# Where six parked tiles leave PSUM, and where the last transposes stand, in a backward pass of one decoder layer

## The chip, the core and the metric

The kernel runs on one core of a Trainium2 chip. The core has five engines with an instruction queue each: TensorE (PE in the profile; its weight loads are PEld), VectorE (DVE), ScalarE (ACT), GpSimd (POOL) and SyncE (SP). They work at the same time and wait for each other through semaphores. Data moves between HBM and the on-chip memory SBUF over 16 DMA engines; here GpSimd and SyncE issue the transfers. TensorE writes only to PSUM, which has 8 banks, and VectorE or ScalarE copy the results from there to SBUF.

The metric is the time of one execution on the device in microseconds, the median of several runs. Lower is better.

## What is computed

The reference is one decoder layer with adaptive layer norm (modulation by a condition vector `c`), attention of one token over the last 4096 positions of a key and value cache, and a gated feed-forward network (FFN); the kernel returns its output and the gradients of ten inputs, for a given output gradient.

```python
def forward(x, k_cache, v_cache, wq, wo, w_gate, w_up, w_down, c, w_mod):
    sa, ca, ga, sb, cb, gb = split6(silu(c) @ w_mod)          # w_mod: 1024 x 6144
    h = layernorm(x) * (1 + ca) + sa
    q = heads(h @ wq)                                         # 32 heads of 128; 4 key/value heads
    p = softmax(q @ k_window.T * 128 ** -0.5)                 # window of 4096 of 65536 positions
    x = x + ga * ((p @ v_window) @ wo)                        # wo: 4096 x 1024
    h = layernorm(x) * (1 + cb) + sb
    x = x + gb * ((sigmoid(h @ w_gate) * (h @ w_up)) @ w_down)  # 1024 -> 3584 -> 1024
    return x

out, grads = vjp(forward)(grad_out)
```

The gradients of the two caches are 64 MB each and zero outside the window, so the kernel has to write about 120 MB of zeros. The gradients of the weights are outer products of a column and a row: a row is broadcast over the 128 partitions once, and each tile of the gradient is that row times one column of scalars.

## The kernel before: the parts that matter

The kernel holds almost everything in one SBUF tile, `arena`, and `ar(offset, size)` is a piece of it, in KiB per partition. Eight matrices `B_t[0..7]` are computed early, from w_q, the attention state and w_o, and must be transposed for a later product (`dh1_ps`). Six of the transposed tiles stay in PSUM banks until the FFN is over ("parked"):

```python
    def park(p, pl, tag):
        BT_ps[p] = pl.tile([P, D], BF16, name="BT_ps", tag=tag)
        for i in range(KD):
            nc.tensor.transpose(BT_ps[p][:, i * P:(i + 1) * P], B_t[p][:, i * P:(i + 1) * P], ident_bf[:, :])
    # ... tiles 0 and 1 in banks "gu" and "x", 2 and 3 in the two of "na", 4 in "pq", 5 in "rq"
    rot[:] = [(psum, "mm")]       # until the end of the FFN, other work has this bank alone
```

`new_ps` and `new_tp` give the next bank of the list `rot` in turn. A side unit transposes one 128 x 1024 tile: eight transposes on TensorE into a bank, then one copy back by ScalarE. A list of such units, `jobs`, is run one by one between the operations of the FFN:

```python
    def tr_unit(blk, dst=None):
        def run():
            tp = new_tp("tp_side")
            for i in range(8):
                nc.tensor.transpose(tp[:, i * P:(i + 1) * P], blk[:, i * P:(i + 1) * P], ident_bf[:, :])
            nc.scalar.copy(out=blk if dst is None else dst, in_=tp[:, :])
        return run

    jobs[:] = [tr_unit(v_nat[:, i // 4, (i % 4) * 1024:(i % 4 + 1) * 1024]) for i in range(16)]
    side(3)
    # ...
    for h in range(HQ):
        jobs.append(tr_unit(wo_t[h // 4][:, h % 4, :]))
    jobs.append(tr_unit(B_t[7]))
    for g in range(G):
        jobs.append(tr_unit(N_sb[:, g * 1024:(g + 1) * 1024]))
```

The FFN's weights come in seven blocks (`NB` is 7). A block reduces each tile with `ttr` on VectorE (for the gradient of the normalized input), then overwrites it with its outer product on ScalarE (the weight's gradient) and stores it:

```python
    for q in range(NB):
        z = Z_FFN[q]
        more = q + 1 < NB
        for j in range(KD):
            w = ug_v[:, q % 2, j // 4, j % 4, :, :].rearrange("p k f -> p (k f)")
            ttr(w, w, dug_b, dh2acc[:, q * KD + j:q * KD + j + 1])
            if j in (0, 2, 5, 6):
                side()
            outer_act(w, h2[:, j:j + 1], dug_b)
            # ... at j == 0: ffn
            if j == 3:
                store_ug(q, 0, 4)
                zero(z[0])
            if j == 5:
                store_ug(q, 4, 2)
        store_ug(q, 6, 2)
        zero(z[1])
        if more:
            # ... front, gates and w_down's part of block q + 1, with three more side() calls
        else:
            zero(z[2] + z[3])
    side(len(jobs))
```

`ug_v` has two halves; odd and even blocks take turns, and the last block (number 6) leaves the odd half unused. Then the gradient goes back through the second layer norm to `dattn`, and through w_o:

```python
    B_t = [ar(o, 2) for o in (40, 42, 44, 152, 154, 156, 62, 60)]
    for p in range(6):
        nc.scalar.copy(out=B_t[p], in_=BT_ps[p][:, :])
    rot[:] = [(psum, "mm"), (pna, "na"), (pgu, "gu"), (ppq, "pq"), (px, "x"), (pna, "na"), (prq, "rq")]
    # ... dh2, dln2
    dx1b, m2 = layernorm_bwd_col(dln2, ln2, rstd2, "ln2b")     # means over partitions by a product on TensorE
    # ...
    mulv(dattn_bf, dx1, ga)
    bcast(dattn_bf, KD, dattn_b, "AV")
    # ...
    do4 = [new_ps("do4") for _ in range(2)]
    for b in range(2):
        for i in range(KD):
            for a in range(4):
                w = wo_t[4 * b + a].rearrange("p a (i d) -> p i a d", i=KD)
                nc.tensor.matmul(do4[b][32 * a:32 * a + 32, :], lhsT=dattn_bf[:, i:i + 1].broadcast_to([P, 32]),
                                 rhs=w[:, i, :, :], start=(i == 0), stop=(i == KD - 1), tile_position=(0, 32 * a))
        nc.scalar.copy(out=do_sb[b], in_=do4[b][:, :])
    # ... dh1_ps: 64 products with the transposed B_t
    def dwo(u):                                                # overwrites wo_t[u], which do4 reads
        for a in range(4):
            outer_dve(wo_t[u][:, a, :], o_col[:, 4 * u + a:4 * u + a + 1], dattn_b)
        nc.gpsimd.dma_start(out=wo_dram(out_5, u), in_=wo_t[u])
    # ... do_ps
    for u in range(4):
        dwo(u)
    bcast(dmod_bf[:, 16:48], 32, dmod_b4, "A")
    # ...
    dwo(4); dwo(5)
    # ... dq_ps: 32 products with the transposed N_sb, then dq_bf; dwo(6), sec(0); c_ps, crow
    sec(1)
    for tb in range(4):
        rebuild_P(tb)
    bcast(dq_bf, HQ, dq_b, "A")
    # ... dwo(7), sec(2), sec(3); dp_ps: products with the transposed v_nat; then
    # the gradients of V, w_q, w_mod and K, each tile stored by GpSimd as soon as it is made
```

In `bcast` each letter names the engine that copies half of the row out of PSUM, in turn: "A" ScalarE, "V" VectorE. `zero(n)` issues `n` stores of zeros, 1 MB each.

Of the kernel before, what the change touches and what calls it, by code (L numbers as in the profile page):

```python
# [20 lines left out]
KD = D // P  # L21
# [4 lines left out]
G = 4  # L26
# [32 lines left out]
def kernel(  # L59
# [26 lines left out]
    nc = tc.nc  # L86
# [13 lines left out]
    def ar(off, size):  # L100
        return arena[:, int(off * KIB):int((off + size) * KIB)]


    def vt(shape, name, dt=FP32):
        return pool.tile(shape, dt, name=name)
# [75 lines left out]
    def new_ps(name="ps"):  # L181
        p, tag = next_pool()
        return p.tile([P, 512], FP32, name=name, tag=tag)
# [4 lines left out]
    def new_tp(name="tp"):  # L188
        p, tag = next_pool()
        return p.tile([P, 1024], BF16, name=name, tag=tag)  # L190
# [7 lines left out]
    def addv(out, a, b):  # L198
        return tt(out, a, b, ALU.add)

    def cp(out, a):
        return nc.vector.tensor_copy(out=out, in_=a)  # L202
# [6 lines left out]
    def ttr(out, w, b, acc):  # L209
        return nc.vector.tensor_tensor_reduce(out=out, in0=w, in1=b, scale=1.0, scalar=0.0,  # L210
                                              op0=ALU.mult, op1=ALU.add, accum_out=acc)
# [28 lines left out]
    def outer_act(out, col, b):  # L240
        return nc.scalar.activation(out=out, in_=b, func=ACT.Copy, scale=col)  # L241
# [51 lines left out]
    def bcast(col_bf, ncols, out_bf, engs):  # L293
        for k, j0 in enumerate(range(0, ncols, 4)):
            ps = new_ps("bc_ps")
            for jj in range(4):
                nc.tensor.matmul(ps[:, jj * P:(jj + 1) * P],
                                 lhsT=col_bf[:, j0 + jj:j0 + jj + 1].broadcast_to([P, P]), rhs=ident_bf[:, :],
                                 start=(jj == 0), stop=(jj == 3), skip_group_check=True)
            o = out_bf[:, j0 * P:(j0 + 4) * P]  # L300
            if engs[k % len(engs)] == "A":
                last = nc.scalar.copy(out=o, in_=ps[:, :])
            else:
                last = cp(o, ps[:, :])
        return last
# [10 lines left out]
    v_nat = ar(96, 32).rearrange("p (g x) -> p g x", g=G)  # L316
    w01_T = ar(128, 16).rearrange("p (n j) -> p n j", n=KD)
    P_bf = ar(144, 8)
    N_sb = ar(144, 8)
# [9 lines left out]
    B_t = [junk if o is None else ar(o, 2) for o in B_off]  # L329
# [108 lines left out]
    jobs = []  # L438
# [5 lines left out]
    def side(n=1):  # L444
        for _ in range(n):
            if jobs:
                jobs.pop(0)()
# [332 lines left out]
    BT_ps = {}  # L780
# [51 lines left out]
# [7 lines that stand above are left out]
# [11 lines left out]
    def load_wd(q, s):  # L850
        nc.sync.dma_start(out=wd_v[:, 2 * s:2 * s + 2, :], in_=wd_dram(B_w_down, q, s))
# [14 lines left out]
    def store_ug(q, j0, n):  # L866
        for k, view in ((0, dwu_view), (1, dwg_view)):
            nc.gpsimd.dma_start(out=ug_part(view, q, j0, n), in_=ug_tile(q, k, j0, n))  # L868
# [42 lines left out]
    park(5, prq, "rq")  # L911
    tr_unit(B_t[6], ar(62, 2))()
    load_wd(0, 1)
    jobs[:] = [tr_unit(v_nat[:, i // 4, (i % 4) * 1024:(i % 4 + 1) * 1024]) for i in range(16)]
    side(3)
    mod_gb((4, 5))
    mulv(dffn_bf, go_col, gb)
# [22 lines left out]
    def gates(q):  # L940
        r, gu = small[q % 2], gu_t[q % 2]
        nc.scalar.activation(out=r["sg"], in_=gu[:, 0:4], func=ACT.Sigmoid)
        nc.scalar.activation(out=r["om"], in_=gu[:, 0:4], func=ACT.Sigmoid, scale=-1.0)
# [23 lines left out]
    def dug_part(q):  # L967
# [4 lines left out]
        for i in range(8):  # L972
            nc.tensor.transpose(tp[:, i * P:(i + 1) * P], r["dug_bf"][:, i:i + 1].broadcast_to([P, P]), ident_bf[:, :])
        nc.scalar.copy(out=dug_b.rearrange("p (s f j) -> p s f j", s=4, j=2),  # L974
                       in_=tp.rearrange("p (s j f) -> p s f j", s=4, j=2))

    for h in range(HQ):
        jobs.append(tr_unit(wo_t[h // 4][:, h % 4, :]))
    jobs.append(tr_unit(B_t[7]))
    for g in range(G):  # L980
        jobs.append(tr_unit(N_sb[:, g * 1024:(g + 1) * 1024]))

    front(0)
    gates(0)
# [11 lines left out]
# [3 lines that stand above are left out]
        for j in range(KD):  # L999
            w = ug_v[:, q % 2, j // 4, j % 4, :, :].rearrange("p k f -> p (k f)")  # L1000
            ttr(w, w, dug_b, dh2acc[:, q * KD + j:q * KD + j + 1])
            if j in (0, 2, 5, 6):
                side()
            outer_act(w, h2[:, j:j + 1], dug_b)
            if j == 0:
                if q == 0:
                    cp(ffn, ffn_ps)
                else:
                    addv(ffn, ffn, ffn_ps)
# [8 lines that stand above are left out]
            front(q + 1)  # L1018
            gates(q + 1)
            side()  # L1020
            hh_ops(q + 1)
            ffn_mm(q + 1, 0)
            wd_ttr(q + 1, 0)
            if q + 2 < NB:
                load_ug(q + 2, 0, 4)
            wd_outer(q + 1, 0)
            zero(z[2])
            if q + 2 < NB:
                load_ug(q + 2, 4, 2)
            side()  # L1030
            ffn_mm(q + 1, 1)
            wd_ttr(q + 1, 1)
            side()
            dug_part(q + 1)
            wd_outer(q + 1, 1)
            if q + 2 < NB:
                load_ug(q + 2, 6, 2)
            zero(z[3])
            if q + 2 < NB:
                load_wd(q + 2, 0)  # L1040
                load_wd(q + 2, 1)
        else:
            zero(z[2] + z[3])
    side(len(jobs))


    B_t = [ar(o, 2) for o in (40, 42, 44, 152, 154, 156, 62, 60)]
    for p in range(6):
        nc.scalar.copy(out=B_t[p], in_=BT_ps[p][:, :])
    rot[:] = [(psum, "mm"), (pna, "na"), (pgu, "gu"), (ppq, "pq"), (px, "x"), (pna, "na"), (prq, "rq")]  # L1050
    dh2 = vt([P, KD], "dh2")
    nc.vector.reduce_sum(out=dh2, in_=dh2acc.rearrange("p (b j) -> p j b", j=KD), axis=AX.X)
# [5 lines left out]
    dattn_bf = vt([P, KD], "dattn_bf", BF16)  # L1058
    mulv(dattn_bf, dx1, ga)
    dattn_b = b1k  # L1060
    bcast(dattn_bf, KD, dattn_b, "AV")
    dmod_bf = vt([P, KM], "dmod_bf", BF16)
    dgb = vt([P, KD], "dgb")
    mulv(dgb, go_col, ffn)
# [37 lines left out]
    def sec(j):  # L1102
        w5 = g_t[j] if j < 6 else sec_t[j][:, 3 * D:4 * D]
        ttr(w5, w5, dmod_b4[:, 3 * D:4 * D], dcs[:, j:j + 1])
        outer_dve(sec_t[j], cs_col[:, j:j + 1], dmod_b4)
        nc.gpsimd.dma_start(out=dwm_view[:, j, 2 * D:6 * D], in_=sec_t[j])
# [56 lines left out]
    for b in range(2):  # L1163
        for hh in range(4):
            nc.tensor.matmul(dov[:, b, :, hh], lhsT=do_sb[b][:, hh * P:(hh + 1) * P], rhs=ident_f[:, 0::32],
                             start=True, stop=True)
    for u in range(4):
        dwo(u)
    bcast(dmod_bf[:, 16:48], 32, dmod_b4, "A")
# [29 lines left out]
    crow = vt([P, 1], "crow")  # L1199
    cp(crow, c_ps[:, 0:1])  # L1200
    sec(1)
    for tb in range(4):
        rebuild_P(tb)
    bcast(dq_bf, HQ, dq_b, "A")
# [106 lines left out]
```

## Time and profile before

| | |
|---|---|
| time, median of 3 runs | 608.62 us (608.2 to 610.81) |
| span of the profiled run | 606.3 us |
| PE, DVE, ACT, POOL busy | 68%, 54%, 47%, 29% |
| bytes moved by DMA | 246.64 MB, mean 407 GB/s |
| HBM read, written | 60.30 MB, 185.60 MB |
| side units' copies by ScalarE (line 837) | 54, of 1009 ns each |
| copies of the six parked tiles (line 1049) | 6, of 1.05 us each |

The busy share of an engine is an average over the whole span, so it doesn't say which stage it limits. The profile also has the span in 40 equal slices, with the share of the DMA engines and the GB/s that they moved, windows of any stretch, and the chain of work that ended last, followed back from the end. "L241" is a line of the kernel, and can be that of a helper: L241 is `outer_act`, L206 the products and scalings of VectorE, L210 `ttr`, L836 and L837 the side units' transposes and copies, L1049 the copies of parked tiles, L1079 `do4`. A DMA share can be over 1, as packets overlap.

### The profile page before, as it was taken

The page shows a single profiled execution, that of the slowest core. Times are in us where ns is not written, and L with a number is a line of the kernel's source. Part 1 is how long each engine was busy: PE and PEld are TensorE (multiplying, and loading weights), DVE is VectorE, ACT ScalarE, POOL GpSimd, SP SyncE. Part 2 cuts the span into 40 slices and gives each one's busy share as a digit, 9 for nine tenths or more (in the row PEclk, how much of TensorE's full clock was granted, in tenths as well). Part 3 has the DMA queues.
Part 4 walks back from the last instruction along what each step waited for, and adds up shares of the span by engine and source line. Part 5 has one row for each costly group of instructions (what it writes and reads, how often), then busy time and mean ns, then how long its engine had stood idle before and what let it go on. Part 6 is the DMA issues. An engine that isn't in the chain of part 4 may idle for free.

```text
span 606.3 us, 11103 instructions
## 1 busy us (share of the span) xinstructions
PE 414.7 (68%) x4587; PEld 278.8 (46%) x4612; DVE 326.2 (54%) x619; ACT 285.4 (47%) x430; POOL 176.4 (29%) x283
## 2 busy tenths in 40 slices
PE   3997789999999989899964535435435356696300
PEld 3995333334344446546543424334434235596200
DVE  3754399999511020160006786685686528998440
ACT  3489514557201024212141875865866953595200
POOL 0002121222222212222331355445445404242230
PEclk9998599999999999999995555555555556755555
DMA  9999999999999999999999999999999998999996
GB/s 350 420 418 422 415 424 417 425 419 419 423 424 427 423 427 419 417 424 429 400 412 392 423 409 412 410 412 412 412 411 409 377 369 309 407 421 424 424 417 270
DMA packets 46899, 246.64 MB, mean 407 GB/s; under 512 B 5565, under 2 KB 5565, under 8 KB 26432
## 3 DMA queue, kind: packets, MB, share of 16 engines
q0 software_dynamic: 37824, 210.78, 91.0%
q1 hardware_dynamic: 8976, 35.14, 16.3%
q8 instruction: 36, 0.59, 0.4%
q14 instruction: 15, 0.12, 0.1%
q10 hardware_dynamic: 48, 0.01, 0.0%
HBM read 60.30 MB, written 185.60 MB: 406 GB/s over the span
## 4 chain that ended last, share of the span: by engine, by line
PE 43%; DMA 26%; DVE 13%; ACT 10%; issue 5%; POOL 0%; ACTq 0%; POOLq 0%; SPq 0%; DVEq 0%
PE b_ps L691 17%; DMA out_dram<-arena 13%; PE n_ps L636 6%; DMA arena<-in_B_w_down_dram 4%; DMA out_dram<-zeros 4%; ACT arena L241 4%; DVE arena L193 4%; DVE arena L206 3%; DMA arena<-in_w_mod_dram 3%; PE t_ps L598 2%; PE ps_kv L1138 2%; DVE arena L210 2%; PE tp_wq L453 2%; PE w_ps L394 1%; PE fold_ps L875 1%
## 5 line engine op out<-in xcount | busy, mean ns | idle before, releaser
L169 POOL DMA_DIRECT2D out_dram<-zeros x112 | 61.7, 553 | 195.7 <-PE q_ps L471 50.8
L691 PE MATMUL b_ps<-arena 128*128 128x512 bf16 x494 | 114.4, 381 | 1.2 <-issue 0.4
L836 PE MATMUL tp_side<-ident_bf,arena 128*128 128x128 bf16 x432 | 53.0, 300 | 59.7 <-ACT arena L837 51.6
L193 DVE TENSOR_TENSOR arena<-arena 128x2048 bf16<-128x2048 bf16 x64 | 76.5, 1223 | 2.3 <-PE n_ps L636 0.3
L691 PEld LDWEIGHTS <-arena 128*128 128x128 bf16 x512 | 49.1, 99 | 56.7 <-issue 4.5
L836 PEld LDWEIGHTS <-arena 128*128 128x128 bf16 x432 | 43.5, 138 | 65.4 <-issue 65.4
L837 ACT COPY arena<-tp_side 128x1024 bf16<-128x1024 bf16 x54 | 54.5, 1009 | 39.3 <-PE tp_side L836 38.9
L210 DVE CUSTOM_DVE_ANT_0 arena<-arena,scr 128x1024 bf16<-128x1024 bf16 x56 | 65.3, 1225 | 9.5 <-ACT scr L974 9.5
L636 PE MATMUL n_ps<-arena 128*128 128x512 bf16 x249 | 65.1, 378 | 6.9 <-DVE arena L193 5.0
L241 ACT ACTIVATE arena<-scr,h 128x1024 bf16<-128x1024 bf16 x56 | 61.3, 1146 | 0.0
L636 PEld LDWEIGHTS <-arena 128*128 128x128 bf16 x256 | 24.6, 97 | 41.6 <-issue 16.2
L868 POOL DMA_DIRECT2D out_dram<-arena x42 | 30.6, 732 | 44.6 <-ACT arena L241 32.9
L202 DVE CAST arena<-b_ps 128x512 bf16<-128x512 f32 x6 | 4.2, 692 | 62.8 <-PE b_ps L691 62.8
L1142 ACT ACTIVATE arena<-ps_kv 128x512 bf16<-128x512 f32 x48 | 26.1, 693 | 23.7 <-PE ps_kv L1138 23.4
L210 DVE CUSTOM_DVE_ANT_0 junk<-arena,b1k 128x1024 bf16<-128x1024 bf16 x28 | 34.3, 1224 | 5.0 <-DMA arena<-in_B_w_down_dram 4.5
L600 ACT CAST arena<-t_ps 128x512 bf16<-128x512 f32 x56 | 30.1, 589 | 12.1 <-PE t_ps L598 12.1
L1138 PE MATMUL ps_kv<-junk,arena 8*128 8x128 bf16 x256 | 27.1, 306 | 12.3 <-DVE arena L206 11.6
L1138 PEld LDWEIGHTS <-arena 8*128 8x128 bf16 x256 | 25.2, 142 | 14.0 <-issue 14.0
L455 ACT COPY arena<-tp_wq 128x1024 bf16<-128x1024 bf16 x23 | 21.8, 1030 | 8.6 <-PE tp_wq L453 8.6
L877 ACT CAST arena<-fold_ps 128x512 bf16<-128x512 f32 x16 | 9.4, 586 | 29.4 <-PE fold_ps L875 29.4
L954 PE MATMUL fg<-hh_bf,arena 128*128 128x1 bf16 x224 | 8.0, 166 | 19.6 <-DMA arena<-in_B_w_down_dram 17.8
L206 DVE TENSOR_SCALAR arena<-arena,cs_col 128x4096 bf16<-128x4096 bf16 (+1 forms) x16 | 16.0, 1017 | 8.9 <-DMA out_dram<-arena 8.8
(296 smaller groups left out, 649.6 us busy)
## 6 DMA issues: line engine op xcount, KB each, us to landing
out_dram<-zeros POOLq DMA_DIRECT2D x112, 1024.0 KB, 13.4
out_dram<-arena POOLq DMA_DIRECT2D x32, 1024.0 KB, 14.3
out_dram<-arena POOLq DMA_DIRECT2D x36, 512.0 KB, 8.9
arena<-in_A_wq_dram SPq DMA_DIRECT2D x8, 1024.0 KB, 19.9
out_dram<-zeros POOLq DMA_DIRECT2D x8, 960.0 KB, 12.5
arena<-in_w_mod_dram POOLq DMA_DIRECT2D x7, 1024.0 KB, 14.7
arena<-in_B_w_down_dram SPq DMA_DIRECT2D x14, 512.0 KB, 8.4
out_dram<-arena POOLq DMA_DIRECT2D x28, 256.0 KB, 9.3
```

The lines of the kernel that those rows point to most:

```text
L169: ins = nc.gpsimd.dma_start(out=region.bitcast(FP32), in_=zeros[:, :])
L193: return nc.vector.tensor_tensor(out=out, in0=a, in1=b, op=op)
L206: return nc.vector.tensor_scalar(out=out, in0=a, scalar1=s1, scalar2=None, op0=op0)
L210: return nc.vector.tensor_tensor_reduce(out=out, in0=w, in1=b, scale=1.0, scalar=0.0, op0=ALU.mult, op1=ALU.add, accum_out=acc)
L241: return nc.scalar.activation(out=out, in_=b, func=ACT.Copy, scale=col)
L600: nc.scalar.copy(out=o, in_=ps)
L636: mm = nc.tensor.matmul(nbank[k][:, :], lhsT=k_nat[:, g, t_ * DH:(t_ + 1) * DH], rhs=vp[:, t_ % 2, 4 * k:4 * k + 4, :].rearrange("p h d -> ...
L691: mm = nc.tensor.matmul(bbank[p][k][:, :], lhsT=a4[:, p, h, :], rhs=wo_t[u][:, a, k * 512:(k + 1) * 512], start=(i == 0 and a == 0), stop= ...
L836: nc.tensor.transpose(tp[:, i * P:(i + 1) * P], blk[:, i * P:(i + 1) * P], ident_bf[:, :])
L837: nc.scalar.copy(out=blk if dst is None else dst, in_=tp[:, :])
L868: nc.gpsimd.dma_start(out=ug_part(view, q, j0, n), in_=ug_tile(q, k, j0, n))
L1138: nc.tensor.matmul(ps[:, t4 * DH:(t4 + 1) * DH], lhsT=rows[32 * g:32 * g + HG, t_ * P:(t_ + 1) * P], rhs=hd[32 * g:32 * g + HG, :], start= ...
```

## The change

The last FFN block gets no side units. ScalarE copies the six parked tiles in their place, into homes in the half of `ug_v` that the last block leaves unused. So `jobs` must be empty by then: four of the 16 transposes of V move behind `c_ps`, ahead of `rebuild_P`, and the four of N move behind the w_o product, ahead of the first `dwo`. The broadcast of `dattn` is copied by VectorE alone. The aim is a shorter way from the last FFN block to the w_o product and the first gradient of w_o.

```diff
-    jobs[:] = [tr_unit(v_nat[:, i // 4, (i % 4) * 1024:(i % 4 + 1) * 1024]) for i in range(16)]
+    vT_unit = [tr_unit(v_nat[:, i // 4, (i % 4) * 1024:(i % 4 + 1) * 1024]) for i in range(16)]
+    jobs[:] = vT_unit[:12]
     side(3)
@@
+    jobs.append(tr_unit(B_t[7]))
     for h in range(HQ):
         jobs.append(tr_unit(wo_t[h // 4][:, h % 4, :]))
-    jobs.append(tr_unit(B_t[7]))
-    for g in range(G):
-        jobs.append(tr_unit(N_sb[:, g * 1024:(g + 1) * 1024]))
+    B_home = [ar(o, 2) for o in (24, 26, 28, 30, 40, 42, 62, 60)]
+
+    def unpark(p):
+        nc.scalar.copy(out=B_home[p], in_=BT_ps[p][:, :])
@@
             ttr(w, w, dug_b, dh2acc[:, q * KD + j:q * KD + j + 1])
-            if j in (0, 2, 5, 6):
+            if more and j in (0, 2, 5, 6):
                 side()
+            if not more and j in (0, 1, 2, 3, 5, 6):
+                unpark((0, 1, 2, 3, None, 4, 5)[j])
             outer_act(w, h2[:, j:j + 1], dug_b)
@@
-    side(len(jobs))
-
-
-    B_t = [ar(o, 2) for o in (40, 42, 44, 152, 154, 156, 62, 60)]
-    for p in range(6):
-        nc.scalar.copy(out=B_t[p], in_=BT_ps[p][:, :])
+    assert not jobs
+
+
+    B_t = B_home
@@
-    bcast(dattn_bf, KD, dattn_b, "AV")
+    bcast(dattn_bf, KD, dattn_b, "V")
@@ after do_ps, ahead of the first dwo
+    for g in range(G):
+        tr_unit(N_sb[:, g * 1024:(g + 1) * 1024])()
     for u in range(4):
         dwo(u)
@@ ahead of rebuild_P
     sec(1)
+    for run in vT_unit[12:]:
+        run()
     for tb in range(4):
         rebuild_P(tb)
```

## The prediction

> **What bounds the kernel now.** I read the page's slices first, then the windows around the one place where they dip, then the chain of waits through it, then ScalarE's timeline there. The slices (40 of 15.16 us each):
>
> ```profile
> PEclk9998599999999999999995555555555556755555
> DMA  9999999999999999999999999999999998999996
> GB/s 350 420 418 422 415 424 417 425 419 419 423 424 427 423 427 419 417 424 429 400 412 392 423 409 412 410 412 412 412 411 409 377 369 309 407 421 424 424 417 270
> ```
>
> The DMA engines are full from end to end, at 400 to 430 GB/s; no compute engine is (page: PE 68%, DVE 54%, ACT 47%). 246.64 MB at about 415 is 594 us of the 606.3 us span. So time can only be won where DMA is not full: slices 31 to 33 (377, 369, 309), about 470 to 515 us, and the ends. The same by stretches (columns: window, then busy us and count for PE, PEld, DVE, ACT, POOL, then granted clock, DMA share, GB/s):
>
> ```profile
> 460.00:475.70 15.70, 7.08 (x80) 5.89 (x81) 13.89 (x29) 9.78 (x12) 4.16 (x7) 0.50 1.11 419
> 475.70:478.00 2.30, 0.00 (x0) 0.00 (x0) 2.30 (x5) 2.30 (x4) 1.67 (x3) 0.50 0.62 228
> 478.00:498.30 20.30, 8.73 (x74) 6.40 (x77) 3.60 (x22) 14.14 (x15) 5.95 (x10) 0.50 1.11 412
> 498.30:502.40 4.10, 4.10 (x109) 2.62 (x101) 3.22 (x8) 1.17 (x2) 0.80 (x1) 0.98 0.00 0
> 502.40:520.00 17.60, 10.76 (x288) 10.18 (x288) 15.14 (x41) 6.13 (x11) 5.85 (x8) 0.58 1.00 365
> 520.00:560.00 40.00, 30.92 (x367) 27.23 (x359) 36.56 (x73) 29.00 (x55) 13.54 (x19) 0.59 1.04 422
> 560.00:600.00 40.00, 6.19 (x56) 5.65 (x55) 13.48 (x19) 4.18 (x7) 9.66 (x15) 0.50 1.01 418
> ```
>
> Two holes: a half-empty dip at 475.7 to 478.0, and 4.10 us with nothing moving (498.3 to 502.4). From 502.4 the share is 1.00, so 365 GB/s there is the speed of those stores (w_o gradients in 2 KB rows), not a third hole. From 520 to 600 DMA is full again. Why is the queue empty at 498.3? The chain of waits for this stretch (start us, us, what):
>
> ```profile
> 479.98 2.19 ACT arena L241 x2
> 482.17 0.91 ACT arena L837
> 483.12 1.03 PE tp_side L836 x8
> ...
> 487.34 1.03 PE tp_side L836 x8
> ...
> 489.30 5.61 ACT arena L1049 x6
> 494.95 1.01 PE bc_ps L297 x8
> 495.96 3.22 PE do L1079 x25
> 499.18 6.79 DVE arena L206 x16
> ```
>
> Block 6's outer products (L241) end at about 482.1. Then four leftover side transposes go one by one through the single bank "mm" (PE 1.03, copy 1.0 each), then six parked tiles leave their banks (L1049), then dattn's broadcast, the w_o product (`do4`, L1079), and only then VectorE may overwrite `wo_t[0]`. Its first store goes out at 501.15 (GpSimd's timeline: 14.56 us idle before it). Meanwhile the five zero stores issued at 483.91 to 486.6 last until 498.3. VectorE's timeline shows what this delays: it ends `ln2b_parts` at 478.98 and gets the means' product only at 488.72, because that small product stands behind the side transposes in PE's order; `dattn_bf` is ready at 489.87, and its broadcast waits until 494.95 because the next buffer in rotation is "rq", the bank of parked tile 5, copied last.
>
> **What the Trainium skill says.** "DMA: Bandwidth & Descriptors", section "Anatomy of one DMA — SWDGE (gpsimd) path": the DMA engines never wait on semaphores; the wait is on the issuing sequencer, and the engines work through what is queued. The trace agrees: GpSimd idles 14.56 us, but DMA is empty only 4.10, the queued zeros covering the rest. "TensorE: Matmul & The Clock Gate", section "What you observe": the clock doubles after about 4 us of sustained matmuls. Here it is 0.5 until the w_o product and 1.0 from about 498.5, after 3.5 us of it: 32 matmuls took 3.22 us, the next 32 about 1.6. "SBUF — State Buffer", section "SBUF: two separate sides": VectorE's two-port modes can keep GpSimd from writing descriptors. Here issues beside VectorE's w_o products took 0.75 to 0.85 us (0.53 to 0.56 for most zero stores), so no long block is visible.
>
> **The change part by part.**
>
> (a) Six copies move into block 6 at j = 0, 1, 2, 3, 5, 6, in place of the four side copies (j = 0, 2, 5, 6). A copy takes 5.61/6 = 0.935 us of ScalarE's time, an outer product 1.045 (3.23 for three, less overlap). Before: ScalarE waits for the first side transpose, starts outer 0 at 470.86, ends outer 3 at about 475.95, and the first gradient store issues at 476.33. After: the first copy needs no PE and starts when `dug_b` is written (468.8), ends 469.7; outer 0 then waits for VectorE's reduction of the same tile (ends 470.04), so starts near 470.15. Up to the end of outer 3 come 4 x 1.045 + 3 x 0.935 = 7.0, so 477.1 in place of 475.95. All three stores of the block come about 1.2 us later (477.5, 480.5, 483.6). The first lies at the dip: DMA is already half empty at 476, so it stays empty longer. Cost on DMA: about +1.1 us. The homes (24 to 30, 40, 42 KiB) held block 5, whose stores issued by 458.6 for these tiles land about 9 us later (page, DMA issues), before 468.8: no wait there.
>
> (b) Gone after block 6: the queue of four side units (482.1 to 489.3, 7.2 us) and six copies (5.6 us). The means' product can run at 479.0; 489.87 - 488.72 = 1.15 us of VectorE gives `dattn_bf` at about 480.8 (was 489.87). Building both kernels and counting buffer rotation, I find the two broadcasts on "na" and "rq"; "rq" is freed by the sixth copy at about 481.1, so nearly no wait. Both broadcast copies now go to VectorE (0.69 each), since ScalarE is busy to 483.2: about 482.8. The product starts near 481.9, cold: 3.3 us for the half that `dwo(0)` waits for. First `dwo` at about 485.2 instead of 499.18: **14 us earlier**. First w_o store near 487.2 instead of 501.15.
>
> (c) The zeros then last to about 498.3 + 1.1 = 499.4, with w_o stores queued since 487. The 4.10 us hole closes: -4.1 us.
>
> (d) Added behind the product: four N units, PE about 1 us and copy 0.935 each, now over several banks: 3.7 us of ScalarE before the dmod broadcast; and four V units ahead of `rebuild_P`, another 3.7. They delay the q-gradient by about 2 us and P by about 4 to 7, while this side is 14 us ahead, so it stays 7 to 12 us ahead of DMA. The 365 GB/s stores hold DMA for 17 us there. No time.
>
> Sum: -4.1 + 1.1 = **-3.0 us**, 608.6 to 605.6; I say 605.5. The 14 us of shorter chain is not the gain: 10 of it lie under zeros which had to be written anyway.
>
> **Rivals.**
>
> Rival 1, the chain counts in full. If 502 to 600 were paced by VectorE, ScalarE and PE, the whole part would move 10 to 14 us: 595 to 598. For it: the page's chain gives PE 43% and DMA only 26%. Against it: from 520 to 600 the DMA share is 1.01 to 1.04, bytes are unchanged, and after 556 GpSimd's timeline shows nearly every issue waiting about 1.9 us for an earlier store. I give it under one in twenty.
>
> Rival 2, the hole comes back later. The added 7.5 us of ScalarE, or the reuse of buffers (the dV tiles need w_o stores landed; the dwq tiles need the early stores landed) could empty the queue between 505 and 535. Then 607 to 609. For it: in-order VectorE and GpSimd, so one late item holds all behind it. Against it: by my count 10 us of data lie ahead of every such wait.
>
> Rival 3, the dip at 476 grows more than I think, because the six copies lengthen block 6, each maybe 1.05 us instead of 0.935, or wait for a store of block 5. At +2 to 3 us the gain shrinks to 1 or 2: 606.5 to 607.5.
>
> Rival 4, the dip does not grow: without side transposes ScalarE starts earlier, and the zero stores ahead cover it: then 604.5.
>
> **Range and chances.** The hole is a firm 4.1; the dip's growth is 0 to 2.5; other shifts of DMA mixing perhaps 1 either way; the three runs of before spread over 608.2 to 610.81. So 603.5 to 607.6. A gain over 2% means below 596.4, which needs rival 1; a loss over 2% would need 12 us of new holes, and nothing in the profile offers that. Chances: 0.03, 0.95, 0.02.
>
> **What would show it.** Right: a DMA window without zero throughput near 498 to 502; the first w_o product of VectorE near 485; the first gradient store of block 6 near 477.5 and a longer dip around 476 to 479; last DMA near 598 instead of 601. Wrong: a new window with low DMA share between 505 and 540 (rival 2); ScalarE's unparking copies with idle time before them waiting on DMA (rival 3); a span shorter by over 8 us with DMA's rate from 520 on above 430 GB/s (rival 1).

## The result, and the profile after

| | before | after |
|---|---|---|
| time, median of 6 runs each | 609.15 us (608.2 to 610.81) | 605.12 us (604.65 to 606.18) |
| ratio, with its 95% interval | | 0.9934 [0.9917, 0.9952] |
| span of the profiled run | 606.3 us | 604.4 us |

The change gains 4.0 us by the medians; the prediction said 605.5 us, 3.1 less than the 608.6 that the kernel before then had. The profiled run of the changed kernel is one of its two slowest (606.17 us), that of before its fastest (608.13 us), so the two traces show only 1.9 of the 4.0 us. I therefore compare them stretch by stretch, and not by their ends.

The page's slices of the changed kernel, each now 15.11 us:

```profile
PEclk9998899999999979979995555555555596755555
DMA  8999999999999999999999999999999999999995
GB/s 351 420 417 421 414 425 417 420 415 420 422 424 425 422 429 419 407 428 414 399 416 398 365 409 415 408 409 414 408 409 414 378 424 413 418 427 424 424 417 226
```

Slices 31 to 33 (counted from 0; about 468 to 514 us) have 378, 424 and 413 GB/s, where before had 377, 369 and 309. Slice 31, the dip in block 6, stayed; the other two were mended. Slice 22 is worse (365 against 423), which is taken up below. Three stretches of the kernel before, then the changed kernel (columns as before: window, busy us and count for PE, PEld, DVE, ACT, POOL, then clock, DMA share, GB/s):

```profile
476.00:484.00 8.00, 2.90 (x24) 2.54 (x24) 2.88 (x9) 7.02 (x8) 5.03 (x8) 0.50 0.95 346
498.00:503.00 5.00, 5.00 (x118) 3.38 (x111) 3.82 (x10) 1.17 (x2) 0.94 (x2) 0.95 0.14 49
503.00:519.00 16.00, 9.16 (x241) 8.58 (x244) 13.54 (x37) 5.13 (x10) 5.70 (x8) 0.57 1.01 365
```

```profile
476.00:484.00 8.00, 2.02 (x18) 1.47 (x22) 6.37 (x20) 8.00 (x9) 3.50 (x5) 0.50 0.94 342
484.00:498.00 14.00, 13.06 (x240) 9.67 (x233) 12.76 (x39) 7.43 (x11) 8.55 (x12) 0.91 1.13 421
498.00:503.00 5.00, 2.03 (x74) 1.76 (x71) 3.07 (x8) 2.25 (x5) 1.56 (x2) 0.71 1.10 415
503.00:519.00 16.00, 12.12 (x234) 9.16 (x234) 13.11 (x35) 11.35 (x16) 4.82 (x6) 0.77 1.04 415
598.00:606.00 8.00, 0.00 (x0) 0.00 (x0) 0.00 (x0) 0.00 (x0) 0.00 (x0) 0.50 0.03 13
```

Two things are to be seen. The hole is gone: 415 GB/s at 498 to 503, where the same window of before moved 49. And the w_o stores at 503 to 519 run at 415, where they ran at 365. The prediction had the first; it took the 365 for the speed of those stores and so had no gain there.

The table turns such windows into time. For each stretch it takes the difference of the rate to that of before, times the length of the stretch, divided by the 422 GB/s that a full stretch moves: the us that a kernel gained on before in that stretch. The gains come from the bytes themselves; from the rounded rates they can differ by 0.2 us in the longest stretches. Four kernels of the experiments stand beside it.

| stretch, us | before, GB/s | after | block 6 only (4) | copies behind block 6 (3) | zero earlier (9) | both (12) |
|---|---|---|---|---|---|---|
| 196 to 324 | 419 | -1.0 | +0.1 | -0.2 | +0.2 | -0.2 |
| 324 to 348 | 407 | -1.6 | -0.9 | -0.9 | -0.6 | -0.8 |
| 348 to 476 (two windows) | 410, 416 | +0.3 | +0.5 | +0.5 | +0.5 | +0.3 |
| 476 to 484, the dip | 346 | -0.1 | -3.4 | +0.9 | +0.9 | +1.5 |
| 484 to 498 | 427 | -0.2 | -1.5 | -0.1 | -0.3 | -0.2 |
| 498 to 503, the hole | 49 | +4.3 | +4.4 | +4.3 | +4.3 | +4.3 |
| 503 to 519, w_o stores | 365 | +1.9 | -0.1 | +2.0 | +2.0 | +2.0 |
| 519 to 590 (three windows) | 418, 423, 422 | +0.1 | -0.1 | -1.9 | 0.0 | +0.1 |

So the changed part, 476 to 519 us, gained 5.9 us: 4.3 by the hole, 1.9 by the rate behind it, -0.3 in block 6 and the stretch after it. From 519 to 590 nothing changed: both kernels are full there. Two losses stand against the 5.9 us in this trace. One is 2.7 us ahead of 348 us. Up to there all kernels of this document but number 6 run the same instructions in the same order, and yet 324 to 348 moves between 353 and 413 GB/s in their traces: variation from run to run, not a cost of the change. The other is the end. After 598 us the changed kernel has almost nothing left to move, but its last packets arrive at 601.6 us: 13 GB/s in the window above, at a DMA share of 0.03, which is half of one of the 16 engines. Before still moved 155 GB/s there and ended at 603.6 us. When 244 of the 246.64 MB have landed, the changed kernel is 3.5 us ahead of before; at the last packet 2.0 are left.

How the compute side moved is seen in the chain of waits of the changed kernel (start us, us, what):

```profile
480.74 0.60 PE tot_ln2b_means L255 x2
...
482.57 1.03 PE bc_ps L297 x8
483.61 4.98 PE do L1082 x57
...
492.07 0.48 PE tp_side L836 x8
492.57 3.76 ACT arena L837 x4
```

The side units and the six copies that stood between block 6 and the broadcast are gone. From the means in VectorE's hands (481.36 in its timeline) to the w_o product (L1082, the former L1079, at 483.61) are 2.2 us, where it was 7.2, from 488.72 to 495.96. VectorE's timeline has its first product for `dwo(0)` at 486.90, where before it was 499.18. The N units (L836, L837) stand behind.

The dip in block 6 is seen in ScalarE's timeline of the changed kernel (start, us, engine, line, operation, tiles, count, idle time before and its releaser):

```profile
470.46 1.02 ACT L984 COPY arena<-BT_ps 128x1024 bf16<-128x1024 bf16 x1
471.86 1.15 ACT L241 ACTIVATE arena<-scr,h 128x1024 bf16<-128x1024 bf16 x1 [0.39 <-DVE dh2acc L210]
472.92 0.99 ACT L984 COPY arena<-BT_ps 128x1024 bf16<-128x1024 bf16 x1
473.81 1.15 ACT L241 ACTIVATE arena<-scr,h 128x1024 bf16<-128x1024 bf16 x1
474.86 1.00 ACT L984 COPY arena<-BT_ps 128x1024 bf16<-128x1024 bf16 x1
475.75 1.15 ACT L241 ACTIVATE arena<-scr,h 128x1024 bf16<-128x1024 bf16 x1
476.80 1.01 ACT L984 COPY arena<-BT_ps 128x1024 bf16<-128x1024 bf16 x1
477.69 2.20 ACT L241 ACTIVATE arena<-scr,h 128x1024 bf16<-128x1024 bf16 x2
...
482.62 2.21 ACT L241 ACTIVATE arena<-scr,h 128x1024 bf16<-128x1024 bf16 x2
```

Copies (L984) and outer products (L241) alternate at 1.94 us a pair, so the first four outer products end at about 478.8 and the first gradient store of the block goes out at 479.15; before, it went out at 476.33. GpSimd's timelines, before and after:

```profile
476.33 1.52 POOL L868 DMA_DIRECT2D out_dram<-arena  x2 [7.45 <-ACT arena L241]
479.15 1.52 POOL L868 DMA_DIRECT2D out_dram<-arena  x2 [8.56 <-ACT arena L241]
```

### The profile page after: what moved, and what is told of

The parts are those of the page before. It is cut to its first block, busy times and chain, and to the rows that moved or that the text cites. A ratio compares the mean times of both kernels' runs of the same rounds, so it can differ in the third digit from the quotient of the medians.

```text
span 604.4 us, 11129 instructions
## 1 busy us (share of the span) xinstructions
PE 415.3 (69%) x4612; PEld 275.5 (46%) x4612; DVE 327.1 (54%) x620; ACT 284.5 (47%) x429; POOL 175.9 (29%) x283
## 2 busy tenths in 40 slices
DMA packets 46899, 246.64 MB, mean 408 GB/s; under 512 B 5565, under 2 KB 5565, under 8 KB 26432
## 4 chain that ended last, share of the span: by engine, by line
PE 36%; DMA 28%; DVE 15%; ACT 8%; issue 8%; POOL 1%; ACTq 0%; POOLq 0%; SPq 0%; DVEq 0%
PE b_ps L691 14%; DMA out_dram<-arena 14%; DVE junk L210 4%; DVE arena L206 3%; ACT arena L241 3%; DMA arena<-in_B_w_down_dram 3%; DMA out_dram<-zeros 3%; DMA arena<-in_w_mod_dram 3%; DMA arena<-in_A_wo_dram 3%; PE n_ps L636 3%; ACT arena L837 2%; DVE arena L210 2%; PE tp_wq L453 2%; PE tp_side L836 2%; DVE arena L193 2%
## 5 line engine op out<-in xcount | busy, mean ns | idle before, releaser
L691 PE MATMUL b_ps<-arena 128*128 128x512 bf16 x512 | 122.4, 393 | 0.7 <-DMA arena<-in_A_wo_dram 0.7
L836 PE MATMUL tp_side<-ident_bf,arena 128*128 128x128 bf16 x432 | 50.9, 297 | 47.4 <-ACT arena L837 40.5
L837 ACT COPY arena<-tp_side 128x1024 bf16<-128x1024 bf16 x54 | 54.0, 1012 | 41.9 <-PE tp_side L836 41.6
L836 PEld LDWEIGHTS <-arena 128*128 128x128 bf16 x432 | 42.3, 137 | 51.9 <-issue 51.7
L241 ACT ACTIVATE arena<-scr,h 128x1024 bf16<-128x1024 bf16 x56 | 61.6, 1147 | 0.4 <-DVE dh2acc L210 0.4
```

Of the source, the lines that this page charges most:

```text
L691: mm = nc.tensor.matmul(bbank[p][k][:, :], lhsT=a4[:, p, h, :], rhs=wo_t[u][:, a, k * 512:(k + 1) * 512], start=(i == 0 and a == 0), stop= ...
```

## Experiments

Each kernel was compared with the kernel before on the same chip; the medians of before were 609.12 us beside numbers 1 to 4, 609.63 beside 5 to 8, 609.29 beside 9 to 11 and 609.2 beside 12. Numbers 7, 8, 10 and 11 have one run each, the others 4 to 19. My theory at first: the time follows from the holes in DMA's work alone, the 365 GB/s behind the hole included, as a consequence of it. Against it stood rival 1 (the earlier compute is worth something by itself) and the reading of the prediction (365 GB/s is the speed of those stores).

### 1. The hole filled with zeros, the compute left late

Two zero stores of the end are issued ahead of the hole instead of behind it (three there instead of one); nothing else changes.

```diff
-Z_END = (1, 1, 1, 0, 0)
+Z_END = (3, 0, 0, 0, 0)
```

> The kernel before with two 1 MB zero stores moved from behind the first w_o stores to ahead of them (three instead of one); no compute instruction moves. Theory (only DMA idle time sets the end): two stores of 2.45 us fill the hole of 4.10 us at 498 to 502, so -4 us if nothing opens later; the two stores are then missing at 511 and 522, so up to 2 or 3 us may come back near 530: 604 to 607 against 609. If the 365 GB/s of the w_o stores came from the hole and not from their rows, they run at about 410 here too, and 2 us more are won. Rival (the chain of PE, ScalarE and VectorE after the FFN paces the end): no change, 609.

Measured: 608.01 us (605.61 to 610.66), ratio 0.9972 [0.9947, 0.9997]; 604 to 607 was expected. Its windows:

```profile
498.00:503.00 5.00, 5.00 (x115) 2.86 (x105) 3.23 (x9) 1.17 (x2) 0.80 (x1) 0.85 1.15 428
503.00:519.00 16.00, 9.53 (x213) 9.21 (x213) 13.40 (x37) 4.11 (x9) 5.20 (x7) 0.71 1.01 369
532.00:548.00 16.00, 13.98 (x178) 12.76 (x178) 15.96 (x21) 13.05 (x27) 5.46 (x8) 0.55 0.83 322
```

The hole is full (428), which is worth 4.5 us at that place, but only 1 to 2 us are left at the end (1.1 by the medians, 1.7 by the ratio). At 532 to 548 a new hole opens (322): the zeros that lay there before are gone, and the compute, 12 us later than in the changed kernel, can't fill it. From 519 to 590 this kernel loses 6.1 us to before, 3.8 of it in that hole. So closing a hole needs both: something to move now, and compute that is early enough when the moved zeros are missed. And the 365 stayed (369) though no full hole lies ahead of it: that part of my theory fell as I had put it.

### 2. The changed kernel, with the hole made again

The zeros of the last block are issued behind the w_o products instead. The compute is as early as in the changed kernel.

```diff
-Z_FFN = [(1, 1, 0, 1)] * 5 + [(1, 1, 1, 1), (1, 2, 1, 1)]
-Z_END = (1, 1, 1, 0, 0)
+Z_FFN = [(1, 1, 0, 1)] * 5 + [(1, 1, 1, 1), (0, 0, 0, 0)]
+Z_END = (0, 7, 1, 0, 0)
```

> The changed kernel with six zero stores moved from ahead of the first w_o store to behind the sixth one; compute is untouched, so the w_o products still start near 487. Theory (the gain is what the early w_o stores and the queued zeros keep DMA from being idle): DMA runs empty between block 6's stores and the first w_o store, 4 to 5 us of holes in all, so 608 to 610, nearly all of the gain lost, and the w_o stores drop to about 365 GB/s again if a hole ahead of them is the cause of that. Rival (the shorter chain is the gain): it stays at 605.

Measured: 610.6 us (609.89 to 612.5), ratio 1.0022 [1.0014, 1.003]. The whole gain is lost, with compute as early as it was. Windows:

```profile
476.00:492.00 16.00, 9.98 (x165) 7.03 (x166) 13.72 (x43) 10.03 (x11) 6.19 (x9) 0.71 0.75 267
492.00:504.00 12.00, 7.67 (x161) 7.32 (x158) 9.57 (x26) 7.68 (x12) 6.25 (x10) 0.65 1.00 355
504.00:520.00 16.00, 7.93 (x181) 7.38 (x182) 7.75 (x24) 7.74 (x9) 3.96 (x7) 0.61 1.13 419
```

The changed kernel moves about 380 GB/s in the first of these (342 for 8 us, 421 for the other 8): (380 - 267) x 16 / 422 = 4.3 us lost in the hole, and (420 - 355) x 12 / 422 = 1.8 us in the slow stretch behind it; 6.1 in sum, 5.5 by the medians. Rival 1 is refuted: 12 us of earlier compute are worth nothing where DMA runs dry. And the slow w_o stores are back, in a kernel that otherwise has them fast.

### 3. The copies behind block 6, the side units still moved away

The opposite half of the change: the six tiles leave their banks after the block, as before, while the N and V units stay behind.

```diff
-            if not more and j in (0, 1, 2, 3, 5, 6):
-                unpark((0, 1, 2, 3, None, 4, 5)[j])
@@
+    for p in range(6):
+        unpark(p)
     B_t = B_home
```

> The changed kernel with the six copies of parked tiles taken out of block 6 and put behind it on ScalarE, as before; no side units in block 6 either, so its ScalarE work is the eight outer products alone. Theory (DMA): the block's first gradient store issues about 4 us earlier than in the changed kernel, so the dip near 480 (about 1.4 us) nearly goes, and the first w_o product about 2 us later costs nothing: 603.5 to 605 against 605.1. Rival (chain): about 2 us slower than the changed kernel, 607.

Measured: 602.95 us (602.59 to 603.09), ratio 0.9891 [0.9875, 0.9908], better than the changed kernel, outside its interval, and better than the 603.5 to 605 expected. ScalarE's timeline in this kernel:

```profile
471.00 9.24 ACT L241 ACTIVATE arena<-scr,h 128x1024 bf16<-128x1024 bf16 x8 [1.30 <-DVE dh2acc L210]
480.15 5.56 ACT L984 COPY arena<-BT_ps 128x1024 bf16<-128x1024 bf16 x6
```

Eight outer products in one go; the first store of the block issues at 475.95 instead of 479.15, and 476 to 484 moves 395 GB/s, where it was 342: 1.0 us. The first w_o product comes at 489.91, three us later than in the changed kernel, and the hole stays closed with 410. What it loses is later, 1.9 us over 519 to 590 in the table: 0.8 at 532 to 548 (401 GB/s), where the compute is only just early enough, and 1.0 at 556 to 590 (409 GB/s, before 422), where the DMA share is 1.01 in both. So the copies inside the block, the most visible part of the change, cost; by number 4 what gains is that the side units left the way (together with the broadcast's copies by VectorE alone, which was not tried by itself). The dip explains 1.0 of the 2.2 us between the medians. The trace's other differences lie ahead of 348 us and at the end, and I can't tell there what is cause and what is variation.

### 4. The copies inside block 6 alone

The kernel before, with the copies taken into block 6 and the side units left where they were, between and behind.

```diff
             if j in (0, 2, 5, 6):
                 side()
+            if not more and j in (0, 1, 2, 3, 5, 6):
+                unpark((0, 1, 2, 3, None, 4, 5)[j])
@@
-    B_t = [ar(o, 2) for o in (40, 42, 44, 152, 154, 156, 62, 60)]
-    for p in range(6):
-        nc.scalar.copy(out=B_t[p], in_=BT_ps[p][:, :])
+    B_t = B_home
```

> The kernel before with only one part of the change: the six copies inside block 6, but the side units stay where they were (four in block 6, four after it). Theory (DMA): block 6's first store comes 3 to 4 us later, so the dip at 476 grows by about as much; the way to the first w_o product is about as long as before, so the hole stays at 2 to 4 us: 609 to 612. Rival (moving the copies is what helps): below 607.

Measured: 609.89 us (608.64 to 611.61), ratio 1.0016 [1.0005, 1.0027]. Windows:

```profile
476.00:484.00 8.00, 2.02 (x16) 1.69 (x16) 3.46 (x11) 8.00 (x9) 2.07 (x3) 0.50 0.47 165
503.00:519.00 16.00, 11.11 (x231) 10.85 (x231) 13.21 (x38) 4.36 (x9) 6.21 (x9) 0.66 1.00 362
```

Here ScalarE is packed: its first store of the block goes out at 480.56, the dip falls to 165 GB/s, and the hole at 498 to 503 is closed only because the zeros behind the block are late as well (issued from 489.81, before from 483.91). The table shows it as a trade: 4.9 us lost in 476 to 498, 4.4 won in the hole, and the w_o stores as slow as before. Half of the change alone is worth nothing.

### 5. The copies in the order in which the banks are needed

Number 3, with the tiles copied so that the banks of the first broadcasts come free first.

```diff
-    for p in range(6):
+    for p in (2, 5, 3, 0, 4, 1):
         unpark(p)
```

> The version with the six copies behind block 6 (602.95), with the copies reordered to parked tiles 2, 5, 3, 0, 4, 1, so that the two banks which dattn's broadcast takes next are free first (there the broadcast waited until 483.02 and 485.76). Theory: the first w_o product comes 3 to 4 us earlier (486 to 487), and the slower stretch of stores near 532 to 548, where the compute had run late, goes: 601 to 602.5. Rival (behind the closed hole nothing of the chain matters any more): no change, 603.

Measured: 603.19 us (602.87 to 604.09), ratio 0.9897 [0.9873, 0.992], the same as number 3, as the rival had it. The broadcast stands at 481.42 and the w_o product at 482.39, and 532 to 548 is mended (423 GB/s, 401 in number 3), and when 244 of the 246.64 MB have landed this kernel is 1.8 us ahead of number 3. But its last 0.25 MB take from 594.7 to 598.3 us, those of number 3 from 596.4 to 598.5. In these two traces what was won in the middle is lost in the last packets. The cause of that end is not settled.

### 6. Number 5, with zeros moved from the middle into the fold

`Z_FOLD` counts the zero stores around the start of FFN block 0: three of them move from behind its first stores to ahead of its first product.

```diff
-Z_FOLD = (0, 4, 3)
+Z_FOLD = (0, 7, 0)
```

> The same as e5, and the three zero stores that follow FFN block 0's first stores are issued ahead of its first product instead. Theory: the weak place at 330 to 336 (the changed kernel's profile shows 145 GB/s in its worst 2 us) is a dry queue before those zeros, so 1 to 2 us less than e5. Rival (the zeros only move, and the queue runs dry at the next store): the same as e5.

Measured: 603.98 us (603.64 to 605.23), ratio 0.9908 [0.9887, 0.9929]: no gain. It was aimed at the weak stretch around 330 us. 328 to 336 rises to 427 GB/s (311 in number 5), but 340 to 344 falls to 244 (415) and 344 to 348 to 314 (404). The hole was only moved, as the rival said.

### 7. Number 2, with the w_o stores issued late (inconclusive)

Meant to let six w_o stores go out in one burst after the last product, so that they run without VectorE's products beside them.

```diff
-        nc.gpsimd.dma_start(out=wo_dram(out_5, u), in_=wo_t[u])
+        if u > 5:
+            nc.gpsimd.dma_start(out=wo_dram(out_5, u), in_=wo_t[u])
@@ behind dwo(5)
+    for u in range(6):
+        nc.gpsimd.dma_start(out=wo_dram(out_5, u), in_=wo_t[u])
```

> The starved version (e2) with the first six w_o stores all issued when the sixth is computed, so that none of them runs while VectorE makes those products; the queue has been dry for some 10 us by then. If the slow w_o stores (365 GB/s in place of 410) come from a queue that ran dry just ahead of them, they are slow here too, about 355 to 370. If they come from VectorE's products running at the same time, they are fast, 405 to 420. The time itself is some 10 us above e2 by the longer hole.

Measured: 610.6 us in one run. Each store still left when its own tile was ready (488.40, 490.10 and so on), since GpSimd had nothing else to wait for: the edit didn't do what it was for, and the run is a repeat of number 2, with 355 to 358 GB/s in the slow stretch. Number 10 does it properly.

### 8. The changed kernel, with 24 products more on VectorE

Is it VectorE's work in SBUF that slows the stores? The 24 products have the form of the w_o products, write to a free place and add nothing to the result.

```diff
     dwo(5)
+    for u in range(24):
+        outer_dve(ar(44, 2), o_col[:, u:u + 1], dattn_b)
```

> The changed kernel with 24 more VectorE products of 128x1024 into an unused piece of SBUF behind the sixth w_o product (about 10 us of VectorE's time, at 498 to 508), so that the w_o stores, which run from 500 on with a full queue, have the same VectorE work beside them as in the kernel before. If that work makes the stores slow: 355 to 370 GB/s from 500 on. If a dry queue does: 405 to 420. The time: within 1 us of the changed kernel if there is 10 us of room behind the hole, up to 5 us more if not.

Measured: 605.36 us in one run. Windows:

```profile
476.00:484.00 8.00, 2.89 (x26) 1.81 (x30) 6.34 (x23) 7.95 (x9) 3.50 (x5) 0.50 0.87 312
500.00:508.00 8.00, 0.00 (x0) 0.00 (x0) 7.43 (x17) 1.72 (x4) 0.29 (x1) 0.56 1.02 412
536.00:540.00 4.00, 4.00 (x44) 4.00 (x43) 4.00 (x5) 4.00 (x9) 2.13 (x3) 0.50 0.73 295
```

VectorE is busy 93% of 500 to 508 with nothing but such products, and the w_o stores run at 412 GB/s beside them. So the products don't slow the stores. The third window shows the room that was left: delayed by some 10 us, the compute no longer keeps up at 536 to 540. The first is a second trace of the changed kernel's dip, as the two kernels are the same up to `dwo(5)`: 312 GB/s here, 342 there.

### 9. The changed kernel, with one zero store earlier

The dip from the other side: one zero store moves from behind block 6 to the end of block 5, ahead of block 6's stores.

```diff
-Z_FFN = [(1, 1, 0, 1)] * 5 + [(1, 1, 1, 1), (1, 2, 1, 1)]
+Z_FFN = [(1, 1, 0, 1)] * 5 + [(1, 1, 1, 2), (1, 1, 1, 1)]
```

> The changed kernel with one 1 MB zero store moved from behind block 6 to ahead of it (behind block 5's last stores). Theory (the dip near 479 to 483, about 1.4 us, is the queue running dry before block 6's late first store): 2.45 us more in the queue close it, 603.5 to 604.2 against 605.1, while the backlog behind block 6 is still long enough. Rival (what is won there is lost again at the end, where single DMA engines finish late): 605.

Measured: 602.67 us (602.24 to 603.87), ratio 0.9894 [0.9875, 0.9912]. The window of the dip:

```profile
476.00:484.00 8.00, 3.40 (x30) 2.04 (x34) 6.27 (x26) 7.44 (x8) 3.75 (x6) 0.50 1.06 395
```

395 GB/s for 342: 1.0 us by bytes, and 2.4 us by the medians, more than I expected. Nothing about the copies was changed, so the dip is a matter of what is queued ahead of the late stores. In its trace the last byte lands at 597.8 us, 3.8 us ahead of the one trace of the changed kernel. By the table 2.2 of these lie ahead of 348 us, where the two kernels are the same, and 1.0 in the dip, so this pair of traces can't say where the rest of the 2.4 comes from.

### 10. Number 2, with the first w_o stores held until the products are done

The proper form of number 7: the first of the six stores also waits for the last product of `dwo(5)`.

```diff
+            prod = outer_dve(wo_t[u][:, a, :], o_col[:, 4 * u + a:4 * u + a + 1], dattn_b)
@@ behind dwo(5), in place of the stores inside dwo
+    for u in range(6):
+        st = nc.gpsimd.dma_start(out=wo_dram(out_5, u), in_=wo_t[u])
+        if u == 0:
+            dep(st, last_prod)
```

> What e7 was meant to do: the starved version (e2), with the first six w_o stores held until VectorE has made the sixth product (in e7 each still went out as soon as its own tile was ready), so none of them runs beside those products. Dry queue ahead makes them slow: 355 to 370 GB/s from about 498 to 514. VectorE's products make them slow: 405 to 420. The time is 7 to 9 us above e2 by the longer hole.

Measured: 620.01 us in one run. DMA is dry from 491 to 499 us (2 GB/s). Then:

```profile
500.00:516.00 16.00, 9.81 (x268) 9.07 (x268) 12.29 (x32) 9.56 (x14) 6.96 (x11) 0.68 1.00 364
517.00:525.00 8.00, 5.83 (x55) 2.96 (x51) 7.93 (x14) 5.26 (x11) 1.61 (x2) 0.80 1.14 424
```

The products for these stores are all done when the first one leaves, six stores are issued together, and they run at 364 GB/s all the same. Neither the products nor the pace of the issue makes them slow. VectorE has other work meanwhile (12.29 of the 16 us), but number 8 shows fast stores beside a busier VectorE. With the next zeros the rate is 424.

### 11. Number 2, with one zero store among the w_o stores

```diff
-Z_END = (0, 7, 1, 0, 0)
+Z_END = (0, 6, 1, 0, 0)
@@
         dwo(u)
+        if u == 0:
+            zero(1)
```

> The starved version (e2) with one of its zero stores put right behind the first w_o store. In the kernel before, in e1, e2 and e4 the slow stores went on until a zero store came up. If one zero store ends it: from about 495 on 405 to 420 GB/s, and about 1.5 us less than e2 (609). If it needs a long queue: still 355 to 370 until the later zeros.

Measured: 608.71 us in one run. Windows:

```profile
490.00:492.00 2.00, 2.00 (x30) 2.00 (x30) 2.00 (x6) 0.45 (x1) 1.09 (x2) 0.98 1.03 369
494.00:506.00 12.00, 7.11 (x158) 6.78 (x156) 9.10 (x24) 5.92 (x11) 4.76 (x8) 0.64 1.02 406
```

The first store runs at 369, then the zero passes (442 at 492 to 494), and the w_o stores that follow it run at 406. One zero store ends the slow stretch. The expectation counts number 1 among the cases, wrongly: no zero store follows there, and the rate stays low, 394 GB/s at 519 to 532.

### 12. The best of both: numbers 5 and 9 together

Copies behind block 6 in the order of number 5, zeros as in number 9.

> e5 (copies behind block 6, reordered) with the zero store of e9 ahead of block 6. In e5 the dip at 476 to 480 is nearly gone (397 GB/s), in e9 too (387). Theory: both mend the same dip, so together they bring at most 0.3 us more: 602.3 to 603.2. Rival (each mends something of its own): 601 to 602.

Measured: **600.85 us (600.47 to 601.7), ratio 0.9858 [0.9836, 0.9881]**, the lowest time of all, 4.3 us below the changed kernel. Windows:

```profile
476.00:484.00 8.00, 2.87 (x26) 1.79 (x30) 6.34 (x23) 8.00 (x9) 5.66 (x9) 0.50 1.12 423
598.00:606.00 8.00, 0.00 (x0) 0.00 (x0) 0.00 (x0) 0.00 (x0) 0.00 (x0) 0.78 0.00 0
```

The dip is closed (423), and nothing is left to move after 598 us; the last byte lands at 596.6. By the table the middle is worth 1.6 us in the dip over the changed kernel; the rest of the 4.3 us is in the end and ahead of 348 us. It was faster than either theory had it, and nearest to the rival: by the ratios number 5 is 0.0037 below the changed kernel, number 9 0.0040, and the two together 0.0076, so their gains simply add up. The dip, which both mend, can't give that twice; what else each of them mends isn't shown.

## Why the prediction was right, and where it was not

**The bound** (DMA full from end to end, time to be won only in its holes): shown. Number 2 has the compute of the changed kernel and a hole, and is slower than before; from 519 to 590 us the changed kernel and before both move 418 to 424 GB/s.

**Step (a), the copies delay block 6, +1.1 us at the dip.** The mechanism was right: a copy and an outer product take 1.94 us a pair (1.98 was taken), the first store comes 2.8 us later than before, 1.7 of it because the whole block started 1.7 us later in this run (its `dug_b` copy at 469.55, before 467.84), so 1.1 by the copies, and 1.2 was predicted. Yet the dip did not grow in this trace: 342 GB/s against 346, -0.1 us. The queue ahead of it ran later too: its last store landed at 480.79 us, before at 479.11. In number 8, the same up to there, the dip did grow: 312 GB/s, -0.6 us. So the term lies between 0.1 and 0.6 in two traces, below the 1.1 predicted. Number 3 shows what the copies cost in the end: 1.0 us at the dip.

**Step (b), the chain.** `dattn_bf` was predicted at 480.8, the first `dwo` at 485.2: measured 482.35 and 486.90, so 1.6 and 1.7 us late, which is the late start of the block. Relative to it the chain is 14.0 us shorter, as predicted. The first w_o store left at 489.48 and not near 487.2: GpSimd was still issuing the five zeros (486.58 to 489.48). With zeros queued this cost nothing. (The prediction's 3.5 us of w_o product before the clock rose at 498.5 are, by its own chain, 2.5 us of it and 1.0 of the broadcast.)

**Step (c), the hole closes, -4.1 us.** Right: -4.3. The last zero store landed at 503.16 us and not at 499.4, and the w_o stores queued since 489.48 followed it without a gap.

**Step (d), the N and V units cost no time.** Right. The N units' copies ran at 492.57 to 496.33 and the V units' at 506.18 to 509.9; the first gradient of V was stored at 525.18 instead of 535.22, so that side is still 10 us ahead. Number 8 takes those 10 us away by other work, and the compute falls behind DMA at 536 us.

**What failed** is a sentence in the first part: "365 GB/s there is the speed of those stores (w_o gradients in 2 KB rows), not a third hole". In the changed kernel the same stores run at 415, which gained 1.9 us that the sum has not. The packets are the same in size (4096 bytes, not 2 KB); in the traces they take 159 to 160 ns in the median in the changed kernel and numbers 3, 5, 6, 8, 9 and 12 and in number 11 after its zero store, and 173 to 175 ns in before and numbers 1, 2, 4, 7 and 10. What divides them is the queue at the first w_o store: in the fast kernels three to five earlier stores of GpSimd's had not landed yet, in the slow ones (with 11) one (1, 2, 4, 11) or none (before, 7, 10). It ends when a zero store passes, at about 519 to 521 us in before and at 492 in number 11. VectorE's products are ruled out by number 8.

The traces have it a second time, later. In numbers 1, 3 and 8 the rate dips again between 532 and 548, when no zero store is left, and from 556 to 590 they stay slower than the kernel before, at the same DMA share (lines of before, 1 and 3; number 8 has 407 GB/s at a share of 1.01):

```profile
556.00:590.00 34.00, 9.07 (x87) 8.37 (x84) 17.48 (x25) 6.57 (x12) 10.30 (x16) 0.50 1.01 422
556.00:590.00 34.00, 13.37 (x129) 12.55 (x128) 20.39 (x29) 9.34 (x16) 10.35 (x16) 0.50 1.01 407
556.00:590.00 34.00, 6.96 (x66) 6.26 (x60) 15.37 (x22) 5.14 (x9) 9.24 (x15) 0.50 1.01 409
```

All other kernels move 420 to 425 there. What the engines do differently after a dry queue is not shown; number 11 gives a remedy, not a cause.

**The sum.** Predicted: -4.1 + 1.1 = -3.0. By bytes in the changed part: -4.3 - 1.9 + 0.3 = -5.9. By the medians: -4.0. That the total came so close is partly luck: two terms missed in the same direction (the dip by 0.5 to 1.0 us, the w_o stores by 1.9), and part of what they gave didn't arrive at the end. Of that part this trace shows 2.7 us ahead of 348 us, which is variation, and the last packets, up to 601.6 us; whether the second belongs to the change stays open. The sign "last DMA near 598 instead of 601" did not come: it was 601.6, and before's last packet came at 603.6.

**The rivals.** Rival 1 is refuted by number 2. Rival 2 (the hole comes back) did not happen in the changed kernel, and did in small in numbers 3 (401 GB/s at 532 to 548) and 8, and fully in number 1 (322). Rival 3 is what number 4 looks like (165 GB/s at the dip), where the side units stayed. Rival 4, the dip that doesn't grow, is nearest to the changed kernel's own trace; number 8's lies halfway to the prediction.

## What to carry to other kernels

When DMA bounds a kernel, shorten a chain only as far as a dip in DMA's rate shows, and count the gain in bytes per stretch: 14 us of shorter chain were 4 us here, and filling the same hole with stores taken from later gave 1 to 2 us, as they were missed 30 us on. Work put into a stage delays that stage's stores: look at what is queued ahead of the first of them, since here one store of 1 MB, issued earlier, was worth as much as leaving the work out. And a rate below the usual at a DMA share of 1.00 is not yet the speed of those transfers; look at the same transfers in another surrounding before it is taken for granted.

## What the runs showed of the hardware that I had not expected

- The same 1 MB stores in 4096-byte packets ran at 355 to 370 GB/s behind a queue that had run (nearly) dry, and at 405 to 420 behind a full one, with the DMA share at about 1.00 or above in both: 173 to 175 ns a packet against 159 to 160. A single store of zeros between them ended it (number 11). After a later dip with no zero store behind it, a lower rate lasted to 590 us: 407 to 409 GB/s in numbers 1, 3 and 8, 420 to 425 in the others.
- The end of a kernel doesn't follow the bulk: the last 0.25 MB took from 597.2 to 601.6 us in the changed kernel and from 594.4 to 596.6 in number 12. Two us that were ahead at 244 MB could be lost there (number 5 against number 3).
- Instructions that are the same in all kernels but number 6 moved between 353 and 413 GB/s in the stretch 324 to 348 us, and the dip of the changed kernel was 342 GB/s in one trace and 312 in another (number 8). One trace against one trace is therefore no measure for a gain of 2 us; medians are, and windows where the difference is far above such variation, as in the hole (49 and 410 to 428).
